# The second feed-forward product as seven half-size block products in fp16

## The chip, the cores and the metric

The kernel runs on one core of a Trainium2 chip. The metric is the time of one execution on the device, in microseconds (us). "TensorE clock" is the clock that the chip granted to the matmul engine, 1.0 being full speed. Each run is named fast or slow: slow when it lies over 1.5% above the fastest run of the same kernel. Unless a slow run is named, all comparisons here use fast runs.

## The reference

Attention over 8 batches of 8 heads (576 positions, 64 channels, a causal mask by blocks of 64), whose output is turned into 4608 rows of 512 channels. Then comes a feed-forward layer with a gate:

```python
x = np.ascontiguousarray(attn_out.transpose(0, 2, 1, 3)).reshape(B * S, H * D)   # 4608 x 512
h = x @ w_in                                                                      # 512 -> 2048
g = h * (1.0 / (1.0 + np.exp(-beta * h)))
return (g @ w_out).astype(np.float32)                                             # 2048 -> 512
```

## The kernel before

The program is laid out by a planner in the kernel file. It gives each operation to an engine, with a priority and an estimated duration, lets a small model run ahead of the chip, and fixes from that the order of every engine's instructions and the semaphores between them. Each engine then works through its list in that order: e9 and e16, two profiles of one program, have the same list of instructions on each engine, though a load landed 2.8 us later in one. TensorE's list is a mixture: attention steps come first, and pieces of feed-forward work stand between them so that TensorE has something to do while it waits for an exponential or a copy. So a change of one operation can shift the whole order.

The rows are handled in nine chunks of 512. For each chunk:

```python
for j in range(NJ):                                   # 16 tiles of the 2048 inner channels
    # TensorE: h.T = w_in.T @ x.T, four matmuls of 512 columns
    z = g.matmul(PS[:, ph.slot, :], w_in[:, c, 128 * j:128 * j + 128], xT[:, c, ...], ...)
    # ScalarE: tanh;  VectorE: (tanh + 1) * h, which frees the bank
    g.activation(th[tt.slot][:], PS[:, ph.slot, :], ACT.Tanh, scale=beta[:, j:j + 1])
    g.scalar_tensor_tensor(out=gT[tg.slot][:, j, :], in0=th[tt.slot][:], scalar=1.0,
                           in1=PS[:, ph.slot, :], op0=ALU.add, op1=ALU.mult)
# ... (cut)
for w, d0, d1 in ...:                                 # four tiles of 128 rows
    for j in range(j0, j1):                           # 16 tiles in pieces of four
        z = g.matmul(PS[:, po.slot, 0:d1 - d0], gT[tg.slot][:, j, 128 * w:128 * w + 128],
                     w_out[:, j, d0:d1], start=(j == 0), stop=(j == NJ - 1))
    # ScalarE: ost = 0.5 * PS, then the store
```

The second loop is what the change rewrites: 64 matmuls of 512 columns in bf16, in one accumulation bank at a time. The last 128 rows of the kernel are cut in two halves so that the end is short. The loads for attention pass through six buffers for q and k (`ST`) and two for v (`Vs`), which GpSimd casts to bf16. Up to 50 us of the plan, idle stretches of TensorE are filled with dummy matmuls of 256 columns (`NFILL, TFILL = 400, 50000.0`).

The softmax here doesn't subtract the row's maximum and nothing guards it: scores larger than these inputs give would overflow.

## Time and profile before

| | kernel before |
|---|---|
| time, median of 3 | 353.59 us (353.36 to 353.8) |
| profiled span | 350.3 us |
| TensorE, VectorE, ScalarE, GpSimd busy | 97, 47, 60, 22% |
| TensorE clock in the profiled run | full speed to the end of the work |

The lines that carry the argument are quoted in the prediction. In a table of stretches, the columns are the stretch in us, its length, the busy time (and number of instructions) of TensorE, its weight loads, VectorE, ScalarE and GpSimd, then the TensorE clock, the transfers' share of their engines and GB/s. This is the emptiest stretch of the kernel before after the first 50 us:

```profile
108.20:111.60 3.40, 2.47 (x18) 1.02 (x15) 1.25 (x4) 2.54 (x3) 1.45 (x2) 1.00 0.93 240
```

TensorE works 2.47 us of 3.40, or 73%.

### The profile page before, as it was taken

What the parts mean: (1) busy time and instruction counts of PE and PEld (TensorE: products, weight loads), DVE (VectorE), ACT (ScalarE), POOL (GpSimd) and SP (SyncE); (2) the same over time, 40 slices, a digit from 0 to 9 for tenths busy, and PEclk for the clock granted to TensorE, in tenths of its full rate; (3) what the DMA queues carried; (4) which work ended last, traced back from release to release, by engine and by line L of the source; (5) the groups of instructions that cost most, each with busy time, mean ns of one, the idle gap of its engine ahead of it and who ended that gap; (6) DMA issues with size and microseconds to landing.
All of it is one profiled execution on the core that took longest, in us unless ns stands there. A gap on an engine that the chain in (4) does not pass through costs nothing.

```text
span 350.3 us, 6832 instructions
## 1 busy us (share of the span) xinstructions
PE 340.2 (97%) x2809; PEld 171.1 (49%) x2753; DVE 163.8 (47%) x371; ACT 211.8 (60%) x315; POOL 78.5 (22%) x112
## 2 busy tenths in 40 slices
PE   7898999999998999999999999999999999999997
PEld 5474455445445445545445444544544444444444
DVE  4758783257123764745425453554343334424300
ACT  2937962496375896687677766768455355444521
POOL 7577260144044044044005300400000000000000
PEclk9999999999999999999999999999999999999999
DMA  7999999989989988999859797861110010010013
GB/s 206 221 239 231 193 174 203 213 202 205 238 207 209 214 189 188 231 217 199 184 146 153 184 210 167 179 127 44 34 62 31 30 62 30 30 60 32 30 37 115
DMA packets 146671, 51.88 MB, mean 148 GB/s; under 512 B 134720, under 2 KB 142160, under 8 KB 146640
## 3 DMA queue, kind: packets, MB, share of 16 engines
q1 hardware_dynamic: 135744, 37.64, 52.7%
q0 software_dynamic: 5568, 4.36, 8.2%
q10 hardware_dynamic: 5328, 9.44, 7.4%
q8 instruction: 22, 0.36, 0.4%
q14 instruction: 9, 0.07, 0.1%
HBM read 36.71 MB, written 9.44 MB: 132 GB/s over the span
## 4 chain that ended last, share of the span: by engine, by line
PE 89%; DVE 4%; ACT 3%; DMA 2%; issue 1%; SPq 0%; POOL 0%; POOLq 0%; ACTq 0%
PE PS L843 35%; PE PS L810 33%; PE PS L668 7%; PE PS L720 7%; PE PS L764 2%; DMA QKT<-QKn 2%; DVE gT L824 2%; ACT th L820 2%; PE PS L494 2%; PE PS L496 1%; ACT E L682 1%; DVE QKT L608 1%; PE PS L600 1%; DVE xq L739 1%; ACT xT L772 0%
## 5 line engine op out<-in xcount | busy, mean ns | idle before, releaser
L810 PE MATMUL PS<-xT,w_in 128*128 128x512 bf16 x576 | 140.8, 380 | 1.7 <-DVE gT L824 0.8
L843 PE MATMUL PS<-w_out,gT 128*128 128x512 bf16 (+1 forms) x592 | 139.8, 374 | 0.0
L824 DVE SCALAR_TENSOR_TENSOR gT<-th,PS 128x512 bf16<-128x512 f32 x144 | 97.2, 684 | 79.8 <-ACT th L820 78.6
L820 ACT ACTIVATE th<-PS,beta 128x512 f32<-128x512 f32 x144 | 97.8, 696 | 59.7 <-PE PS L810 58.9
L682 ACT ACTIVATE E<-PS 128x1024 bf16<-128x1024 f32 x93 | 92.0, 1029 | 27.6 <-PE PS L668 27.4
L843 PEld LDWEIGHTS PS<-w_out,gT 128*128 128x128 bf16 x592 | 55.3, 98 | 61.8 <-issue 2.1
L810 PEld LDWEIGHTS PS<-xT,w_in 128*128 128x128 bf16 x576 | 53.0, 98 | 63.3 <-issue 2.1
L855 ACT ACTIVATE ost<-PS 128x512 f32<-128x512 f32 (+1 forms) x37 | 21.7, 589 | 41.6 <-PE PS L843 41.6
L630 POOL CAST QKn<-ST 128x640 bf16<-128x640 f32 x48 | 34.7, 722 | 51.5 <-DMA ST<-in_k_dram 30.4
L668 PE MATMUL PS<-QKT 64*128 64x192 bf16 (+4 forms) x328 | 37.0, 297 | 1.6 <-DVE xq L739 1.0
L543 POOL CAST Vn<-Vs 128x2560 bf16<-128x2560 f32 (+2 forms) x11 | 18.5, 1684 | 85.8 <-DMA Vs<-in_v_dram 85.6
L720 PEld LDWEIGHTS PS<-Vn,E 128*128 128x128 bf16 x930 | 31.8, 97 | 6.5 <-issue 0.2
L720 PE MATMUL PS<-Vn,E 128*128 128x65 bf16 x930 | 32.8, 193 | 0.0
L688 DVE MEMSET E<- 64x64 uint32 x62 | 6.9, 112 | 47.2 <-ACT E L682 46.6
L668 PEld LDWEIGHTS PS<-QKT 64*128 64x128 bf16 (+1 forms) x328 | 13.4, 95 | 30.7 <-issue 15.2
L739 DVE TENSOR_TENSOR xq<-PS,inv 128x640 bf16<-128x640 f32 x32 | 26.3, 823 | 0.9
L608 DVE COPY QKT<-PS 128x576 bf16<-128x576 bf16 x16 | 11.8, 754 | 3.3 <-PE PS L600 3.1
L732 DVE RECIPROCAL inv<-PS 128x10 f32<-128x10 f32 x32 | 7.0, 218 | 12.7 <-PE PS L720 12.6
L591 POOL CAST QKn<-ST 96x768 bf16<-96x768 f32 x14 | 11.6, 830 | 3.3 <-DMA ST<-in_k_dram 2.4
L774 DVE COPY xT<-PS 128x64 bf16<-128x64 bf16 (+2 forms) x40 | 9.6, 285 | 5.6 <-PE PS L764 5.5
L690 DVE MEMSET E<- 64x128 uint32 x31 | 5.1, 165 | 14.8 <-ACT E L682 13.8
L764 PE MATMUL PS<-identB,xq 128*128 128x128 bf16 (+1 forms) x100 | 10.5, 216 | 0.3 <-DVE xq L739 0.3
(44 smaller groups left out, 76.1 us busy)
## 6 DMA issues: line engine op xcount, KB each, us to landing
out_dram<-ost ACTq DMA_DIRECT2D x35, 256.0 KB, 2.6
Vs<-in_v_dram SPq DMA_DIRECT2D x28, 256.0 KB, 4.2
ST<-in_q_dram SPq DMA_DIRECT2D x48, 128.0 KB, 2.8
ST<-in_k_dram SPq DMA_DIRECT2D x48, 128.0 KB, 2.9
ST<-in_q_dram SPq DMA_DIRECT2D x8, 288.0 KB, 6.6
ST<-in_k_dram SPq DMA_DIRECT2D x8, 288.0 KB, 7.0
w_in<-in_moe_w_in_dram POOLq DMA_DIRECT2D x4, 512.0 KB, 11.0
w_out<-in_moe_w_out_dram POOLq DMA_DIRECT2D x4, 512.0 KB, 10.9
```

The lines of the kernel that those rows point to most:

```text
L543: return g.tensor_copy(Vn[t.slot][:, 0:n, g0:g1, 0:64], Vs[ts.slot][:, 0:n, g0:g1, :])
L630: return g.tensor_copy(QKn[tn.slot][:].rearrange("p a w n -> p (a w n)")[:, 640 * (2 * a + w):][:, 0:640] .rearrange("p (t h d) -> p t h d ...
L668: z = g.matmul(o, QKT[tqk.slot][r, p, 1, 128 * t:128 * t + m], x)
L682: return g.activation(E3[es_(te)][:, g0, :, :], PS[:, ps.slot:ps.slot + 2, :], ACT.Exp, scale=0.125)
L720: z = g.matmul(o, eblk(te, t, i, h), Vn[Tv.slot][:, t, 2 * c + h, 0:65], start=(t == 0), stop=(t == i))
L739: return g.tensor_tensor(xq[tx.slot][:].rearrange("p i (h d) -> p h i d", h=2), both(pv, 0, 64), x, ALU.mult)
L764: z = g.transpose(PSb[:, px.slot, 128 * i:128 * i + r], xq[tx.slot][0:r, i, :], identB[0:r, 0:r])
L810: z = g.matmul(PS[:, ph.slot, :], w_in[:, c, 128 * j:128 * j + 128], xT[:, c, row % RX:row % RX + RC], start=(c == 0), stop=(c == 3))
L820: return g.activation(th[tt.slot][:], PS[:, ph.slot, :], ACT.Tanh, scale=beta[:, j:j + 1])
L824: return g.scalar_tensor_tensor(out=gT[tg.slot][:, j, :], in0=th[tt.slot][:], scalar=1.0, in1=PS[:, ph.slot, :], op0=ALU.add, op1=ALU.mult)
L843: z = g.matmul(PS[:, po.slot, 0:d1 - d0], gT[tg.slot][:, j, 128 * w:128 * w + 128], w_out[:, j, d0:d1], start=(j == 0), stop=(j == NJ - 1))
L855: return g.activation(ost[to.slot][:, 0:n], PS[:, po.slot, 0:n], ACT.Copy, scale=0.5)
```

## The change

The intent is to do the second product with fewer multiplications. A chunk's product A·B (A is 512x2048, B is 2048x512) is split into quarters and computed as seven half-size products instead of eight, in Winograd's form of Strassen's method:

- S1 = A21+A22, S2 = S1−A11, S3 = A11−A21, S4 = A12−S2, per chunk, on VectorE;
- T1 = B12−B11, T2 = B22−T1, T3 = B22−B12, T4 = B21−T2, once;
- p1 = A11·B11, p2 = A12·B21, p6 = S2·T2, p7 = S3·T3, p5 = S1·T1, p3 = S4·B22, p4 = A22·T4;
- C11 = p1+p2, C12 = p1+p6+p5+p3, C21 = p1+p6+p7+p4, C22 = p1+p6+p5+p7.

The products p1, p6, p5, p3 add up in one bank, which is read out after each of them; p7 and p4 share another. The first chunk keeps the plain product. The values and weights become fp16, meant to give the sums more bits. The sums lie over two of the q/k buffers and one v buffer, so later loads have fewer. The core of the diff:

```diff
+f16 = mybir.dt.float16
+        FAST = range(1, NRC)
+        OV = sb("OV", [128, 5120], f32)                 # lies over ST[4:6] and Vs[1]
+        TW = {k: OVh[:, k - 2] for k in (2, 3, 4)}
+        SW = {k: OVh[:, k + 1] for k in (2, 3)}
-        gT = [sb(f"gT{i}", [128, NJ, RC], bf16) for i in range(2)]
+        gT = [sb(f"gT{i}", [128, NJ, RC], f16) for i in range(2)]
-        w_out = sb("w_out", [128, NJ, DM], bf16)
+        w_out = sb("w_out", [128, NJ, DM], f16)
 ... (cut)
+                tw[k] = P.op("DVE", dve_t(1024), mk(lambda g, o=o, x=x, y=y: g.tensor_tensor(o, x, y, ALU.subtract)),
+                             deps=old + list(tw.values()), prio=0.6)            # four weight sums, once
 ... (cut)
+                return P.op("DVE", dve_t(SZ * HC / 2), mk(lambda g: g.tensor_tensor(
+                    fo(), fx(), fy(), op)), deps=deps, tiles=tiles, prio=prio)  # eight sums a chunk
 ... (cut)
+                for w in range(2):                       # one product: 2 row tiles x 8 tiles, 256 columns
+                        for j in range(HJ):
+                            x = g.matmul(PS[:, ps.slot, HM * w:HM * w + HM], fa()[:, j, 128 * w:128 * w + 128],
+                                         fb()[:, j, :], ...)
 ... (cut)
+            p1 = prod(Z, lambda: G(0, 0), lambda: quad(w_out, 0, 0), lo + wl, [], True, False)
+            z1 = evac(Z, oz, p1)                          # ScalarE
+            p2 = prod(W, lambda: G(0, 1), lambda: quad(w_out, 1, 0), hi + wh, [], True, True)
+            c11 = evac(W, oz, p2 + [z1], add=oz)          # VectorE, adds
 ... (cut: p6, p7, p5, p3, p4 in this order, each read out in turn)
+            if r in FAST:
+                fast(r, row, tg, gs)
+                continue
-            for w, d0, d1 in [(w, 0, DM) for w in range(4 if r < NRC - 1 else 3)] + (
-                    [] if r < NRC - 1 else [(3, 0, DM // 2), (3, DM // 2, DM)]):
+            for w, d0, d1 in [(w, 0, DM) for w in range(4)]:
```

## The prediction

> **What bounds the kernel now.** I read the page first (busy shares, slices, chain), then the chain of work in order of time, then the busy time of each engine in chosen stretches, then the timeline of the end.
>
> From the page of the kernel before:
>
> ```profile
> PE 340.2 (97%) x2809; PEld 171.1 (49%) x2753; DVE 163.8 (47%) x371; ACT 211.8 (60%) x315; POOL 78.5 (22%) x112
> ...
> PE 89%; DVE 4%; ACT 3%; DMA 2%; issue 1%; SPq 0%; POOL 0%; POOLq 0%; ACTq 0%
> ...
> L843 PE MATMUL PS<-w_out,gT 128*128 128x512 bf16 (+1 forms) x592 | 139.8, 374 | 0.0
> L824 DVE SCALAR_TENSOR_TENSOR gT<-th,PS 128x512 bf16<-128x512 f32 x144 | 97.2, 684 | 79.8 <-ACT th L820 78.6
> ```
>
> TensorE is busy 97% of the span and carries 89% of the chain that ended last. L843, the second feed-forward product that the change rewrites, is 35% of that chain. But the 374 ns of one matmul is a latency of pipelined work, so what a matmul costs has to come from spacing. The chain in order of time gives it: each row chunk of 512 rows ends in the same piece, and the pieces repeat exactly.
>
> ```profile
> 249.22 4.32 PE PS L843 x20
> ...
> 276.85 4.32 PE PS L843 x20
> ...
> 304.47 4.32 PE PS L843 x20
> ...
> 332.10 15.59 PE PS L843 x88
> ```
>
> The period is 27.63 us. A chunk has 64 matmuls of the first product and 64 of the second, all with 512 columns, so one costs 27.63 / 128 = **215.9 ns**, with not a nanosecond of waiting in the sum. The end of the kernel also has 32 matmuls with 256 columns (the last output rows are cut in halves). In the timeline of the end:
>
> ```profile
> 331.94 15.74 PE L843 MATMUL PS<-w_out,gT 128*128 128x512 bf16 x88
> ...
> 347.72 0.38 ACT L855 ACTIVATE ost<-PS 128x256 f32<-128x256 f32 x1 [1.31 <-PE PS L843]
> ```
>
> The last of the 88 starts some 15.47 us after the first (15.74 less its own 0.27). 56 of the gaps are wide ones, 56 x 0.2159 = 12.09; the other 31 take 3.38 us, or **109 ns** each. So half-width matmuls, each with its own weight load (98 ns in the page), keep their pace: the load stays hidden.
>
> The stretches show where TensorE has slack and how full VectorE is (columns: PE, PEld, DVE, ACT, POOL busy us):
>
> ```profile
> 40.00:80.00 40.00, 38.59 (x340) 19.61 (x332) 21.29 (x50) 24.82 (x38) 13.26 (x14) 1.00 1.03 199
> 80.00:120.00 40.00, 39.07 (x356) 19.63 (x344) 16.65 (x45) 24.64 (x35) 11.05 (x14) 1.00 0.99 215
> 120.00:160.00 40.00, 40.00 (x377) 19.91 (x364) 23.78 (x64) 30.30 (x46) 13.60 (x15) 1.00 0.93 206
> ...
> 276.85:304.47 27.62, 27.62 (x129) 12.54 (x128) 11.00 (x16) 13.38 (x20) 0.00 (x0) 1.00 0.10 39
> ```
>
> From 120 us on TensorE never stops; before, it loses 2.3 us in 80 while the transfers are full (DMA share 1.03 and 0.99). Attention and its loads end near 248 us, and over three and a half chunks of feed-forward work are then left, so slower loads in the middle would be hidden. VectorE has room everywhere: 60% at its fullest, 40% late.
>
> [...]
>
> **The change part by part**, per chunk, for eight of nine chunks.
>
> TensorE. Removed: 64 wide matmuls, 64 x 215.9 = 13.82 us. Added: seven products, each of 2 row tiles x 8 k-tiles with 256 columns, 112 x 109 = 12.21 us. Saving 1.61 us, not the full eighth (1.73)[...]. Eight chunks: 12.9 us at most. Fp16 should cost no more than bf16.
>
> VectorE. Added: eight sums of 1024 fp16 elements. [...]one is an estimated 690 ns; eight are 5.5 us. Four evacuations move to it, each like the 684 ns row of L824: 2.7. Together 8.3 us a chunk, 66 in all, and once four weight sums of 1.22 us, 4.9. VectorE goes from 164 to some 235 us, 69% of the new span; a late chunk from 11 to 19.3 us of 26; around 120 to 160 us, where a chunk takes some 34 us, from 60% to some 84%. It does not become the bound, but matmul banks will be freed a little later.
>
> ScalarE. Three evacuations for four, 0.6 us less a chunk. Neutral.
>
> Buffers. The new sums lie over two of six q/k staging buffers and one of two v buffers, which later loads then lack. Before, the casts wait for the loads (QKn for k 30.4 us, Vn for v 85.6), not the loads for the casts, so this should show little, except early.
>
> Banks. One accumulating bank is held nearly the whole chunk and a second half of it, where before one output bank was held at a time. While attention lasts, four banks serve feed-forward work, so the first product often has two. One use of a bank is matmuls 0.86 + tanh 0.70 + product on VectorE 0.68, with gaps some 2.5 us, so two banks supply one tile per 1.25 us; TensorE needs one per 1.6 (late) to 2. Just enough: I allow 1.5 us of stalls in all.
>
> Where the saving doesn't arrive. Chunk 1's product runs near 88 to 112 us, when TensorE has nothing but this product to fill with until the next batch's attention is through; I give away half of it, 0.8. In the last chunk, the sequence p5, read of the bank, p3 has a wait of some 0.9 us with no next chunk to fill it (perhaps a left-over of chunk 7); the last evacuation is 0.75 us on VectorE in place of 0.38 on ScalarE; and the last store is 256 KB instead of 128 (2.6 for 1.9 us in the page's issues). So of its 1.6 about 0.5 remains.
>
> Sum: chunks 2 to 7 give 6 x 1.61 = 9.7; chunk 1 0.8; the last 0.5; together 11.0. Less stalls of 1.5: 9.5. 353.6 - 9.5 = 344.1 us.
>
> **The rivals.** (a) **VectorE becomes the bound**: [...] Against it: the rate of the xT copies. Blocking by GpSimd casts (13.6 of 40 us busy there) is the milder form. It would eat 5 to 10 us: 349 to 354. (b) **Banks and in-order waits**: partial sums are read between products, so a late evacuation stops TensorE, which is in order. For it: two or three free banks in the attention stages. Against: late chunks have all eight, and between the products of one chunk lie those of the next. Up to 5 us: 349. (c) **Starved by transfers**: fewer staging buffers while DMA is full. For it: the DMA share of 1.0 to 120 us. Against: the large stock of feed-forward work after 160. It could lose chunks 1 and 2 and some more: 347. (d) **Nothing lost**: 353.6 - 12.9 = 340.7.
>
> **Range and chances.** I weigh the plain sum with small stalls 0.65, (d) 0.1, (a) to (c) 0.25 together. That gives 344.1, range 340.8 to 350.0. Faster by over 2% means below 346.5: 0.74. Within 2%: 0.23. Slower: 0.03.
>
> **What would show it.** In the chain, late chunks with a period of 26.0 us, not 27.63; if it is more, TensorE waits for VectorE or ScalarE and names the line. 896 matmuls with 256 columns. The fp16 sums at 690 ns in the groups by shape; 1.2 us would mean rival (a). TensorE's idle time in 40 to 120 us up from 2.3 by about 1 to 2, and under 1 us from 120 to 250; more with a releaser in VectorE means (b), in DMA or casts (c). The end, from the last tanh to the last store, no more than half a us shorter. The prediction is wrong above all if half-width fp16 matmuls don't keep 109 ns over long runs, or if VectorE's queue delays the products that free the banks.

What the trace of the kernel before has for these estimates, by shape: two matmuls of 256 columns cost 2.1 ns more than one of 512 (2 x 109 against 215.9). The 16-bit copies to xT took 283 ns for 256 elements and 420 for 512, or 0.54 ns an element; at this pace a sum would take an estimated 694 ns for 1024 elements and 1.24 us for 2048. Two f32 operations of VectorE took 684 ns for 512 elements (L824) and 823 for 640 (L739); at their pace a sum of 1024 would take an estimated 1.24 us, which is rival (a). The profile of e1 later had 695 ns for the sums within `gT` and 1.22 us for the weight sums.

## The result

The changed kernel took 350.64 us in the median of five runs (349.75 to 356.78, the highest a slow run), against 353.64 us (353.36 to 354.52) for the kernel before in the same rounds. The ratio of the fast runs is 0.9892 (95% interval 0.985 to 0.9935), which counts as the same within 2%. A ratio here is the mean time of one kernel's fast runs over the mean of the other's fast runs of the same rounds, so it isn't quite the ratio of the medians. The measured 350.64 lies outside the predicted range of 340.8 to 350.0, and 6.5 us above the predicted 344.1. The prediction was wrong. In two later batches the same kernel took 349.57 and 348.28 us in the median, beside 352.94 and 353.83 for the kernel before. These two lie inside the range, but the gain, 3.0, 3.4 and 5.6 us in the three batches, is well under the predicted 9.5 in each.

The profile taken with this result was of the slow run. I read a second profile of the same kernel (350.70 us, span 348.9), the first of the experiments. From its page: busy times, the clock in 40 slices, the shares of the chain that ended last, and three groups.

```profile
PE 331.4 (95%) x3177; PEld 207.5 (59%) x3121; DVE 225.1 (65%) x463; ACT 212.2 (61%) x314; POOL 79.6 (23%) x110
...
PEclk9999999999999998999999999999999999999999
...
PE 78%; DVE 5%; ACT 5%; DMA 4%; SPq 3%; POOL 2%; issue 2%; ACTq 0%; POOLq 0%
...
L879 PE MATMUL PS<-w_out,gT 128*128 128x256 f16 x512 | 65.5, 273 | 0.7 <-ACT ost L893 0.7
...
L896 DVE SCALAR_TENSOR_TENSOR ost<-PS,ost 128x512 f32<-128x512 f32 x24 | 16.4, 685 | 18.0 <-PE PS L879 16.2
L846 DVE TENSOR_TENSOR OV<-gT 128x1024 f16<-128x1024 f16 x32 | 24.5, 774 | 1.1 <-PE PS L879 0.6
```

TensorE's share of the chain fell from 89% to 78%: the end is now reached through more waits on other engines. VectorE stands at 225 us, near the predicted 235, and is no bound. One slice has a lower TensorE clock. The sums at L846 take 774 ns in the mean, not 690.

The late chunks are exactly as predicted. From the chain in order of time (start, length, engine, what, line, count) and the table of stretches:

```profile
277.56 5.24 PE PS L879 x48
...
303.60 5.24 PE PS L879 x48
...
329.63 11.37 PE PS L879 x104
341.68 3.68 PE PS L879 x32
```

```profile
277.56:303.60 26.04, 26.04 (x178) 17.19 (x177) 17.61 (x28) 13.39 (x20) 0.00 (x0) 1.00 0.12 41
```

The period is 26.04 us, for 27.63 before, and TensorE doesn't stop in it. So a narrow fp16 matmul costs (26.04 − 64 x 0.2159) / 112 = 109 ns, and each full chunk saves 1.59 us. The saving is real; it was lost elsewhere. To see where, I added up TensorE's lost time in each trace: the distances between the starts of consecutive matmuls, less the usual distance of that pair of kinds (215.9 and 109 ns within the feed-forward work; between kinds, the lower quartile over the traces). Stretches at half clock count as lost too. For two profiles of the changed kernel and, for later use, one of a kernel with other filling (e13):

| us lost, by time of the start | before | changed, e1 | changed, e17 | e13 |
|---|---|---|---|---|
| to 40 us (loads, start) | 8.5 | 9.5 | 8.7 | 8.2 |
| 40 to 80 | 2.1 | 2.1 | 2.1 | 1.3 |
| 80 to 120 (chunk 1's product) | 1.4 | 2.4 | 3.9 | 1.6 |
| 120 to 140 | 0.2 | 4.3 | 1.8 | 0.9 |
| 140 to 240 | 1.0 | 1.9 | 1.8 | 2.7 |
| 240 to 330 | 0.0 | 1.3 | 1.1 | 0.1 |
| 330 to the last matmul | 0.0 | 0.9 | 0.9 | 0.9 |
| sum | 13.2 | 22.3 | 20.3 | 15.6 |
| last matmul's start to the end of the span | 2.9 | 3.8 | 3.8 | 3.8 |
| span | 350.3 | 348.9 | 346.9 | 343.4 |

The changed kernel saves 12.9 us of matmuls at full pace (560 at 215.9 ns and 32 at 109 make 124.4 us; 64 and 896 make 111.5) and loses 7.1 to 9.1 us more in holes, 0.9 of it in the tail, 0.2 to 1.0 at the start, and most of the rest between 80 and 140 us and around 240. Another 0.96 us goes to a longer end. Some 1.5 us of both differences I can't place; it lies in the switches between kinds of matmul, which this reckoning takes as given.

The largest hole of e1, from its timeline (start, length, engine, line, operation, and the idle time before it with its releaser):

```profile
125.77 2.32 POOL L558 CAST Vn<-Vs 128x2560 bf16<-128x2560 f32 x1 [12.35 <-DMA Vs<-in_v_dram]
...
125.84 2.79 DVE L846 TENSOR_TENSOR OV<-gT 128x1024 f16<-128x1024 f16 x1
...
128.94 1.08 PE L737 MATMUL PS<-Vn,E 128*128 128x65 bf16 x30 [1.66 <-DVE E L707]
```

One cast of v starts on GpSimd, and 0.07 us later a sum starts on VectorE. The sum takes 2.79 us instead of 0.69. Behind it in VectorE's list stands a small memset of the exponentials (L707), on which TensorE's next attention step waits, so TensorE stops for 1.66 us. Then comes the second part:

```profile
127.10:130.50 3.40, 1.74 (x38) 1.26 (x38) 2.97 (x6) 1.30 (x4) 2.55 (x3) 1.00 0.92 200
130.50:133.90 3.40, 3.40 (x8) 0.94 (x8) 2.06 (x5) 1.83 (x3) 1.45 (x2) 0.50 0.66 147
```

TensorE was busy only half of one stretch of 3.4 us (1.74 of 3.40), and in the next one it gets half its clock: 8 wide matmuls took the time of 16, a further 1.7 us. In e17 the same happens around the spot that was emptiest before the change:

```profile
108.20:111.60 3.40, 1.76 (x34) 1.08 (x28) 1.90 (x7) 1.35 (x2) 1.44 (x2) 1.00 1.10 297
111.60:115.00 3.40, 3.20 (x34) 2.24 (x35) 1.36 (x5) 1.05 (x2) 1.45 (x2) 0.50 1.24 242
```

And the end of e1, with ScalarE reading the bank between p5 and p3:

```profile
341.02 0.60 ACT L893 ACTIVATE ost<-PS 128x512 f32<-128x512 f32 x1 [2.02 <-PE PS L879]
341.65 0.69 DVE L896 SCALAR_TENSOR_TENSOR ost<-PS,ost 128x512 f32<-128x512 f32 x1 [1.68 <-ACT ost L893]
...
341.68 1.05 PE L879 MATMUL PS<-w_out,gT 128*128 128x256 f16 x8 [0.69 <-ACT ost L893]
...
345.38 0.69 DVE L896 SCALAR_TENSOR_TENSOR ost<-PS,ost 128x512 f32<-128x512 f32 x1 [3.04 <-PE PS L879]
```

TensorE waits 0.69 us for the read of p5, and after the last product there is an addition of 0.69 us on VectorE and a 256 KB store. That is the wait I had seen coming, but 0.9 + 0.96 us of it in all, more than the chunk's whole saving of 1.6.

### The profile page after: what moved, and what is told of

It reads as the page before. It is cut to its first block, busy times and chain, and to the rows that moved or that the text cites.

```text
span 354.6 us, 7617 instructions
## 1 busy us (share of the span) xinstructions
PE 332.2 (94%) x3140; PEld 209.7 (59%) x3121; DVE 227.1 (64%) x463; ACT 212.6 (60%) x314; POOL 80.4 (23%) x110
## 4 chain that ended last, share of the span: by engine, by line
PE 75%; DVE 6%; DMA 6%; ACT 4%; SPq 3%; issue 3%; POOL 2%; POOLq 0%; ACTq 0%
PE PS L946 31%; PE PS L879 26%; PE PS L737 6%; PE PS L685 5%; PE PS L982 4%; ACT th L956 2%; ACT E L699 2%; DMA ST<-in_q_dram 2%; DMA QKT<-QKn 2%; DVE gT L960 2%; DMA Vs<-in_v_dram 2%; PE PS L781 2%; SPq L532 2%; DVE gT L846 1%; DVE w_out L828 1%
## 5 line engine op out<-in xcount | busy, mean ns | idle before, releaser
L960 DVE SCALAR_TENSOR_TENSOR gT<-th,PS 128x512 f16<-128x512 f32 x144 | 97.0, 683 | 43.8 <-ACT th L956 43.3
L879 PE MATMUL PS<-w_out,gT 128*128 128x256 f16 x512 | 65.5, 273 | 0.7 <-ACT ost L893 0.7
L879 PEld LDWEIGHTS PS<-w_out,gT 128*128 128x128 f16 x512 | 48.5, 98 | 14.4 <-ACT ost L893 1.5
L685 PE MATMUL PS<-QKT 64*128 64x512 bf16 (+4 forms) x328 | 38.0, 303 | 6.5 <-ACT E L699 3.2
L893 ACT ACTIVATE ost<-PS 128x512 f32<-128x512 f32 x32 | 19.2, 600 | 26.4 <-PE PS L879 26.3
L879 PE MATMUL PS<-OV 128*128 128x256 f16 x256 | 34.4, 282 | 0.4 <-DVE OV L828 0.4
L879 PEld LDWEIGHTS PS<-OV 128*128 128x128 f16 x256 | 25.4, 101 | 8.6 <-DVE OV L828 0.5
L896 DVE SCALAR_TENSOR_TENSOR ost<-PS,ost 128x512 f32<-128x512 f32 x24 | 16.4, 685 | 18.1 <-PE PS L879 16.2
L846 DVE TENSOR_TENSOR OV<-gT 128x1024 f16<-128x1024 f16 x32 | 22.7, 716 | 1.1 <-PE PS L879 0.6
L879 PE MATMUL PS<-OV,gT 128*128 128x256 f16 x128 | 16.6, 273 | 0.0
```

What stands on the lines that cost most here:

```text
L685: z = g.matmul(o, QKT[tqk.slot][r, p, 1, 128 * t:128 * t + m], x)
L846: return P.op("DVE", dve_t(SZ * HC / 2), mk(lambda g: g.tensor_tensor(fo(), fx(), fy(), op)), deps=deps, tiles=tiles, prio=prio)
L879: x = g.matmul(PS[:, ps.slot, HM * w:HM * w + HM], fa()[:, j, 128 * w:128 * w + 128], fb()[:, j, :], start=first and w == 0 and j == 0, st ...
L893: return P.op("ACT", act_t(DM) + 80, lambda g, e: g.activation(ost[to.slot][:], PS[:, ps.slot, :], ACT.Copy, scale=0.5), deps=deps, tiles= ...
L960: return g.scalar_tensor_tensor(out=gT[tg.slot][:, j, :], in0=th[tt.slot][:], scalar=1.0, in1=PS[:, ph.slot, :], op0=ALU.add, op1=ALU.mult)
```

## The experiments

The theory after this reading: **VectorE's queue and the clock.** The sums, lengthened by casts that run at the same time, hold up small attention steps on VectorE; TensorE, which is in order, stops (1.66 us in e1); and a stop that empties one stretch of 3.4 us (1.74 us busy in e1) is followed by one at half clock. Rivals (these are new ones; the prediction's have letters): **staging**, fewer buffers for q, k and v, so that loads come late; **chunk 1**, whose product is the only filling around 100 us, so that starting one chunk later would give all back; and **the tail** alone. The runs came in five batches, each with its own runs of the kernel before.

### The first batch: repeat, undo, and cut the sums

**e1_after_again** is the changed kernel, unaltered.

> The changed kernel unaltered, for a profile in the fast state. All theories: about 350.2 us, 3 us under the kernel before. The changeover theory (the loss of some 6 us sits between 80 and 130 us, where the first weight sums and chunk sums queue on VectorE with GpSimd casts) expects TensorE idle there to be about 5 us more than before, and under 1.5 us more elsewhere; the spread theory (VectorE too full in the whole attention stage) expects it evenly from 80 to 250 us.

It took 349.57 us in the median of four runs (347.94 to 350.70), ratio 0.9881 (0.9821 to 0.9942). So the result repeats. Its profile is read above.

**e2_plain_all** keeps fp16, the overlaid buffers and the fourth output buffer, but makes no chunk of seven products:

```diff
-        FAST = range(1, NRC)
+        FAST = range(NRC, NRC)
 (and the last rows cut in halves, as before)
```

> No chunk with the seven products, but all else of the change stays: fp16, the sums' room laid over two q/k staging buffers and one v buffer (nothing is written there), four output buffers. The staging theory (the lost buffers cost the missing 6 us) expects 358 to 360 us, 5 to 6 over the kernel before. The changeover and the spread theories expect 353 to 354.5, as before.

354.48 us, ratio 1.0031 (0.9963 to 1.0099), correct. Fp16 in place of bf16 costs nothing that shows. The interval is too wide to size the buffers; e8 repeats it.

**e3_tiny_weight_sums** cuts the four weight sums to two columns each and leaves the order of all instructions as it was. The result is wrong.

```diff
-g.tensor_tensor(o, x, y, ALU.subtract)
+g.tensor_tensor(o[:, :, 0:2], x[:, :, 0:2], y[:, :, 0:2], ALU.subtract)
 (the products read quarters of w_out where they read T2, T3, T4)
```

> Wrong result on purpose. Order of all instructions and waits as in the changed kernel; only the four weight sums are cut to 2 columns of 256 (16 elements for 2048), and the products read the raw quarter of the weights. Changeover theory, in the form that the weight sums are the culprit: 345 to 347 us, some 4 us faster than the changed kernel. Spread and staging theories: within 1 us of the changed kernel, 349 to 350.5.

349.15 us, ratio 0.9884 (0.9835 to 0.9934): no gain over e1. The length of the weight sums isn't what was lost; the expected gain was a miss. A half-clock stretch remained, at 112.6 us.

**e4_tiny_all_sums** cuts the per-chunk sums to two columns too, with the same order, and is wrong.

```diff
-                    fo(), fx(), fy(), op))
+                    fo()[:, :, 0:2], fx()[:, :, 0:2], fy()[:, :, 0:2], op))
```

> Wrong result on purpose. As the one with small weight sums, and all sums of activations are cut to 2 columns as well (8 elements for 1024), so VectorE is freed of all sums with the order unchanged. Spread theory: 343 to 345 us, near the 344 that the prediction had. Changeover theory with the weight sums as culprit: no more than 1 us below the run with small weight sums. Staging theory: 349 to 350, no gain.

346.98 us, ratio 0.9832 (0.9779 to 0.9885), 2.6 us less than e1. So in this batch the length of all the sums together looks worth some 2 to 3 us, but the intervals overlap, and the unaltered kernel reached the same ratio (0.9833) on another chip in e17: this is not shown. But even with sums of almost no length the kernel doesn't come to 344: a half-clock stretch followed the hole at 108 to 112 us here as well, and one of the sums shows that a cast can lengthen even a sum of eight elements:

```profile
126.30 1.62 DVE L846 TENSOR_TENSOR OV<-gT 128x8 f16<-128x8 f16 x1
```

Eight elements took 1.62 us; the mean of these small sums is 0.25 us. A cast of v had begun at 125.59 and lasted 2.32 us, and the sum ended with it.

### The second batch: contention, the first chunk, GpSimd, staging

**e5_memset_sums** puts memsets of the same length in place of the sums. They read no operand in SBUF, and no lengthening shows in them: both groups of 32 have a mean of 688 ns, and each of the four for the weight sums took 1225 ns.

```diff
-mk(lambda g: g.tensor_tensor(fo(), fx(), fy(), op))
+mk(lambda g: g.memset(fo()[:, :, 0:189], 0.03))
```

> Wrong result on purpose. Order and waits of the changed kernel; each sum (weights and activations) is a memset of about the same length, some 0.7 us for a sum of activations, so VectorE is as busy as in the changed kernel but reads nothing from SBUF for the sums[...]. Theory that contention with the casts is what the sums cost: 346 to 347 us, at least as fast as the run with all sums small (347.0), because there even small sums waited for casts (one took 1.6 us). Theory that it is VectorE's occupancy: 349 to 350, as the changed kernel.

350.36 us (348.44 to 353.23), ratio 0.9915 (0.9878 to 0.9951). That is no better than the changed kernel, so lengthening by casts alone can't be the cause. The profile shows two half-clock stretches, after stretches with TensorE busy for 58 and 51%. The holes are there with sums of plain length.

The hole at 108 to 112 us doesn't depend on the sums' length at all. The least busy 3.41 us between 100 and 115 us are 46% full in e1, e3, e4, e5 and e17 alike, and in e17 no sum runs there. TensorE waits until VectorE has scaled the attention output (`xq`). Before the change, four wide matmuls of chunk 1's product stood in this wait. First the kernel before, then e17:

```profile
107.54 1.03 PE L843 MATMUL PS<-w_out,gT 128*128 128x512 bf16 x4
108.88 0.39 PE L668 MATMUL PS<-QKT 64*128 64x512 bf16 x2 [0.31 <-DVE xq L739]
```

```profile
107.81 1.08 PE L737 MATMUL PS<-Vn,E 128*128 128x65 bf16 x30
110.07 0.39 PE L685 MATMUL PS<-QKT 64*128 64x512 bf16 x2 [1.18 <-DVE xq L756]
```

So this hole is missing filling, and not a sum in the way. Whether chunk 1's shorter product or the new order takes it away wasn't tried apart.

**e6_from_third** starts one chunk later.

```diff
-        FAST = range(1, NRC)
+        FAST = range(2, NRC)
```

> The seven products from the third chunk on, the second chunk plain. Theory that the second chunk's saving never arrives (TensorE runs dry near 108 us whatever the second chunk costs, because the third waits for its batch) and that the first sums make it worse: 348 to 349.5 us, as fast as the changed kernel or up to 1.5 us faster, with TensorE idle between 80 and 140 us by some 2 us less. Rival, that each chunk's saving counts: 351 us, 1.6 slower.

352.82 us, ratio 0.9986 (0.9962 to 1.0009): 3 us worse than the changed kernel, where one chunk's saving is at most 1.6. The chunk-1 rival in its simple form missed. The holes did not go away; the two deepest, 1.9 us at 110.5 and 2.1 us at 239.1 by the reckoning of lost time, were each followed by a half-clock stretch (from 112.9 and 242.6). All six runs had a clock of 0.990 or lower.

**e7_pool_sums** moves the per-chunk sums to GpSimd, except in the last chunk.

```diff
-                return P.op("DVE", dve_t(SZ * HC / 2), ...
+                return P.op("POOL" if r < NRC - 1 else "DVE", 1100 if r < NRC - 1 else dve_t(SZ * HC / 2), ...
```

> The sums of activations on GpSimd in place of VectorE in all chunks but the last. If contention and occupancy on VectorE cost some 2.5 us, and a sum takes GpSimd about 1.1 us (an estimate from its casts, 0.72 us for 640 elements): 347 to 348 us. If the sums are slower than 2 us there, they will hold the casts up and the products that need them: over 350.

357.49 us, ratio 1.0078 (1.0036 to 1.012), worse than before the change. The sums there took twice the time that I had planned for:

```profile
L846 POOL TENSOR_TENSOR OV<-gT 128x1024 f16<-128x1024 f16 x28 | 60.3, 2154 | 44.5 <-DVE gT L960 26.9 <-PE PS L879 16.0
```

The groups have 2.12 to 2.24 us, or some 2.1 ns an element; the 1.1 us was an estimate from the casts, which take 1.13 ns an element (0.72 us for 640). And the contention only changed sides: three of the four weight sums on VectorE, beside sums on GpSimd, took 2.5 to 3.1 us instead of 1.22.

**e8_plain_all_again** is e2 with more rounds.

> A repeat of the run without the seven products, for a narrower interval: 354.5 was measured beside 352.9 for the kernel before. Theory that the two lost staging buffers and the lost v buffer cost 1 to 3 us: a ratio of 1.003 to 1.008, and a hole in TensorE of about 1 us between 240 and 260 us where it waits for the last transposed loads. Theory that they cost nothing: a ratio within 0.998 to 1.002.

353.87 us, ratio 1.0007 (0.9974 to 1.0039). In time the smaller staging costs less than the scatter. In the trace it does show. The order of TensorE's instructions is that of the kernel before, instruction for instruction, and there are two new holes, at 231 and 237 us. The second:

```profile
238.96 0.39 PE L685 MATMUL PS<-QKT 64*128 64x512 bf16 x2 [1.14 <-DMA QKT<-QKn]
```

TensorE lost 2.2 us in 220 to 240 us, against 0.3 before. The same wait on the transposing transfer of the last batch is in e1 (1.13 us at 244.6). So the staging rival is right in kind for some 1 to 2 us, late in attention, and no more.

### The third batch: fill the hole, start later, mend the tail

**e9_fill_the_hole** lets the planner put dummy matmuls into idle stretches up to 135 us of the plan. It adds 23 of 256 columns, 20 of them near 108 to 113 us, and its order of everything after differs.

```diff
-        NFILL, TFILL = 400, 50000.0
+        NFILL, TFILL = 600, 135000.0
```

> The changed kernel with 20 dummy matmuls of 256 columns (2.2 us at 109 ns) put among the attention work near 108 to 113 us, where TensorE ran dry in the profiles. Theory that holes of some 2 us make the clock drop to half for 3.4 us and that this costs up to 1.7 us: full clock from 100 to 120 us, and 348 to 349 us if no other hole drops it. Rival, that the clock plays no part: 349.6 or slower by the dummies. The order behind them shifts, so a second drop near 130 us may stay; the clock of the profiled run will say.

348.02 us (345.78 to 349.2), ratio 0.9825 (0.9787 to 0.9863), correct, and the clock was between 0.998 and 1.0 in all six runs.

**e10_from_fourth** starts with the fourth chunk, when there is more feed-forward work in stock.

```diff
+        FAST = range(3, NRC)
```

> The seven products from the fourth chunk on, so that the weight sums and the first sums come after 140 us, when TensorE has a stock of feed-forward work. Stock theory (until some 140 us TensorE has nothing to put in the place of a late attention step, so that each delay on VectorE becomes a hole, and a hole halves the clock): no drop of the clock, holes between 80 and 140 us as in the kernel before (1.6 us by the sum of gaps, against 6.6 in the changed kernel's fast profile), and 346.5 to 348.5 us although 3.2 us of saving are given up. Rival, each chunk's saving counts wherever it is: 352.8.

351.33 us, ratio 0.9925 (0.9886 to 0.9964), a miss. The stretch from 80 to 140 us is then nearly as before the change (1.8 us lost, for 1.6), but 2.2 us are lost in new holes between 180 and 200, where the four weight sums now sit, again against a cast of v:

```profile
184.24 2.32 POOL L558 CAST Vn<-Vs 128x2560 bf16<-128x2560 f32 x1 [18.40 <-DMA Vs<-in_v_dram]
...
184.71 2.92 DVE L828 TENSOR_TENSOR OV<-w_out 128x2048 f16<-128x2048 f16 x1
```

The disturbance moves with the first chunk of seven products; starting later doesn't avoid it. Three of the six runs had a clock of 0.99.

**e11_from_fourth_plain_last** is e10 with the last chunk plain, its end in halves. The quarter B12 is changed in place, so its result is wrong (relative error 0.14). I take the timing to stand; that the values do not matter to it isn't shown by a run.

```diff
+        FAST = range(3, NRC - 1)
```

> As the run from the fourth chunk, and the last chunk plain with its end halved as in the kernel before. Tail theory (the last chunk's saving of 1.6 us is eaten by a hole of 0.85 us and a longer last evacuation and store of about 1.0): within 0.7 us of the run from the fourth chunk. Rival: 1.6 us slower than that.

349.55 us, ratio 0.9882 (0.9854 to 0.991), all six runs at full clock. The three full-clock runs of e10 have a mean of 349.95, these six of 349.69. So nothing of the last chunk's 1.6 us shows, though three and six runs spread over 1.5 and 2.3 us can't exclude a part of it. The traces say the same: its tail takes back 0.9 + 0.96 us.

**e12_from_fourth_split_end** keeps the last chunk's seven products, but puts p7 and p4 into two banks in halves, so that additions and stores of the end are half as large.

```diff
+  Y = (P.tile("P1"), P.tile("P1"))     # in the last chunk (this cut is shortened)
+  for w in range(2):                   # the last two additions and stores, in halves; the last store by SyncE
+      P.op("DVE", dve_t(HM), ... ost[to.slot][:, c], in0=PS[:, ps[w].slot, c] ...)
```

> As the run from the fourth chunk, with the last chunk's final two evacuations and stores in halves over two banks, so that the end is 256 columns on VectorE (about 0.42 us) and a store of 128 KB. If the longer last evacuation and store cost about 1.0 us: 0.7 to 1.0 us faster than the run from the fourth chunk, and the time from the last matmul's start to the end near 2.9 us where the changed kernel has 3.8.

350.56 us (two of the six runs slow; the four fast ones have a mean of 349.95), ratio 0.9889 (0.9856 to 0.9921), so no gain over e10 that shows. The last matmul's start to the end took 4.17 us, against 3.67 in e10: the last store, of 128 KB, was issued at 343.73 and took 3.0 us to land. A miss.

### The fourth batch: what the filling does

**e13_two_column_fill** is e9 with dummies of 2 columns in place of 256, so that they fill an order but hardly any time.

```diff
+  g.matmul(PS[:, tf.slot, 0:2], identB[:], identW[:, 0:2])     # planned after 60 us
```

> Order and waits exactly as in the run with dummy matmuls in the hole, but the 20 dummies near 108 to 113 us have 2 columns for 256, so TensorE is idle there again. Theory that the clock is what that run gained: the clock drops to half once near 110 to 117 us and the time goes back up by 1 to 2 us, to 349 to 350. Rival, that the changed order behind the dummies gained it: no change, 348.

348.29 us, ratio 0.9811 (0.9752 to 0.987). The gain stayed, so it isn't the dummies' work that does it; I had expected it to go. What the profile shows is another order, in which the hole at 108 to 112 us holds other work: TensorE was busy 2.57 of the 3.40 us from 108.2 (0.49 of it only the small dummies), for 1.76 in e17. Its profiled run took 345.23 us, the fastest of its six and 1.1 above the prediction; the median is 4.2 above it.

**e14_fill_tiny_sums** joins e9 and e4 (wrong).

> Wrong result on purpose. Dummy matmuls in the hole, and all sums (weights and activations) cut to 2 columns, the order as in the run with the dummies. If holes left by VectorE's sums and the clock's drop are separate causes that add: 345 to 346 us, 2 to 3 under the run with the dummies, and within 2 us of the 344.1 that the prediction had. If they are one cause: 348.

348.20 us, ratio 0.9821 (0.9753 to 0.989). With this order the sums' length is worth nothing that shows; the two gains don't add up.

**e15_fill_plain_last** is e9 with a plain last chunk, and one more VectorE operation that turns B12 back, so its result is right.

```diff
+        FAST = range(1, NRC - 1)
+                    quad(w_out, 0, 1), quad(w_out, 0, 1), quad(w_out, 0, 0), ALU.add)), deps=[tw[1], tw[2], *used], ...
```

> Correct. Dummy matmuls in the hole, and the last chunk plain with its end halved as before (one more sum on VectorE turns the changed quarter of the weights back). A candidate for the best version. Tail theory: 346.5 to 348, the same as the run with the dummies or up to 1.5 us faster. If the last chunk's saving counts: 349.6.

349.17 us, ratio 0.9809 (0.9738 to 0.9879; the median includes two slow runs). The same as e9 again: nothing to be had in the tail either way.

**e16_fill_again** is the same program as e9.

> The run with the dummies again, beside the three others on their chip: 348 us, full clock through all runs.

348.52 us (one of the six runs slow), ratio 0.9829 (0.9768 to 0.989). It repeats e9 in time, and the two profiles show how much is chance. First e9, then e16, around 96 us, with the same list of instructions on each engine:

```profile
95.61 1.22 DVE L828 TENSOR_TENSOR OV<-w_out 128x2048 f16<-128x2048 f16 x1
...
98.04 2.47 POOL L558 CAST Vn<-Vs 128x2560 bf16<-128x2560 f32 x1 [12.53 <-DMA Vs<-in_v_dram]
```

```profile
95.21 2.38 POOL L558 CAST Vn<-Vs 128x2560 bf16<-128x2560 f32 x1 [11.82 <-DMA Vs<-in_v_dram]
95.33 3.34 DVE L828 TENSOR_TENSOR OV<-w_out 128x2048 f16<-128x2048 f16 x1
...
98.73 2.88 PE L879 MATMUL PS<-OV 128*128 128x256 f16 x16 [1.51 <-DVE OV L828]
```

In e9 the load of v landed 2.8 us later, and the weight sum, 1.22 us long, was over before the cast began. In e16 the cast was first by 0.12 us, the sum took 3.34, TensorE waited for it, and the clock followed:

```profile
96.10:99.50 3.40, 1.51 (x17) 1.01 (x16) 3.30 (x4) 2.59 (x5) 1.57 (x2) 1.00 1.10 257
99.50:102.90 3.40, 3.40 (x38) 2.85 (x36) 0.99 (x3) 0.60 (x1) 2.88 (x4) 0.50 1.01 211
```

The spans were 346.0 and 349.0 us. This is the clearest pair: one program, one meeting of a cast and a sum more, 3 us. (By the reckoning of lost time, 3.2 us of it lie between 80 and 120 us; other stretches differ by up to 1.4 us either way and nearly cancel.) That the cast comes first was set by a transfer's landing, 2.8 us apart in the two, which the same order of instructions did not fix.

### The fifth batch: is any version better?

**e17_after_third** is the changed kernel again, and **e18_fill_plain_last_again** is e15, both on a third chip.

> The changed kernel once more, beside the candidate for the best version on the same chip: 349 to 350.5 us and a ratio near 0.989, with one or two drops of the clock in most runs.

> The candidate for the best version again (dummy matmuls among the attention work near 108 to 113 us, last chunk plain): 1 to 2.5 us faster than the changed kernel of the same rounds, 347 to 349.

e17: 348.28 us (346.30 to 350.81), ratio 0.9833 (0.9786 to 0.988). e18: 348.45 us, ratio 0.9845 (0.9793 to 0.9897). So the filling that looked 1 to 2 us better in other batches isn't better here. No version beats the changed kernel in a way that repeats. An interval that crosses 0.98 in the table leaves open whether that run is faster by 2% or the same.

| run | median us | ratio to before | 95% |
|---|---|---|---|
| changed kernel (three batches) | 350.64, 349.57, 348.28 | 0.9892, 0.9881, 0.9833 | see above |
| e2, e8 plain, fp16 and smaller staging | 354.48, 353.87 | 1.0031, 1.0007 | .9963–1.0099, .9974–1.0039 |
| e3 weight sums cut | 349.15 | 0.9884 | .9835–.9934 |
| e4 all sums cut | 346.98 | 0.9832 | .9779–.9885 |
| e5 memsets for sums | 350.36 | 0.9915 | .9878–.9951 |
| e6 from the third chunk | 352.82 | 0.9986 | .9962–1.0009 |
| e7 sums on GpSimd | 357.49 | 1.0078 | 1.0036–1.012 |
| e9, e16 filled | 348.02, 348.52 | 0.9825, 0.9829 | .9787–.9863, .9768–.989 |
| e13 filled, two columns | 348.29 | 0.9811 | .9752–.987 |
| e10, e12 from the fourth | 351.33, 350.56 | 0.9925, 0.9889 | .9886–.9964, .9856–.9921 |
| e11 from the fourth, last plain | 349.55 | 0.9882 | .9854–.991 |
| e14 filled, sums cut | 348.20 | 0.9821 | .9753–.989 |
| e15, e18 filled, last plain | 349.17, 348.45 | 0.9809, 0.9845 | .9738–.9879, .9793–.9897 |

### The clock, read over all profiles

No run was made for this; it is a reading of the twenty traces there are. In a trace with two half-clock stretches, their starts lie a whole number of 3.413 us apart, to 0.02 us: 98.38 and 115.44 in e5 (5 times), 112.86 and 242.56 in e6 (38 times). The profile of the slow run has three, 6.827, 3.413 and 3.413 us long, from 14.40, 103.15 and 120.21 us (26 and 5 times). So in these traces the clock changes on a fixed grid of 3.413 us. For 19 of the profiles a half-clock stretch, if only that after the end of the work, gives the position of the grid, and I took TensorE's busy share in every cell of it after 38 us:

| busy share of a cell | cells | followed by a half-clock cell |
|---|---|---|
| up to 0.514 | 13 | 12 |
| 0.52 to 0.60 | 7 | 1 |
| over 0.60 | all others | 0 |

So TensorE needn't be idle for a whole cell: of the 13 cells with TensorE busy for up to 51%, 12 were followed by 3.41 us at half clock. The clock records of the kernel before and of the slow run have two states, full and half.

This may also be why equal programs differ. Taking every position of a 3.41 us window, the least busy one between 100 and 115 us is 73% busy before the change, and 46% in five profiles of the unaltered order (e1, e3, e4, e5, e17). Whether a cell falls on that hole differs from run to run with the grid's position. In e1 none did (the cell there had 58%), and the hole at 127 us was caught, with half clock from 130.5; in e17 one did, with half clock from 111.6. Among the 14 fast runs of the changed kernel, the five at a clock of 0.998 or more have a mean of 347.8 us, the eight at 0.995 a mean of 350.0, and one at 0.988 took 349.8. One stretch of 3.41 us at half clock makes a mean clock of 0.995 over 348 us.

## Why the prediction was wrong

By its own steps:

- **A narrow matmul at 109 ns: right.** 896 of them, a late period of 26.04 us against the foretold 26.0, TensorE without a stop in late chunks. Fp16 cost nothing that shows (e2 and e8: ratios of 1.0031 and 1.0007), and the results were right (e1, e17) although a bank is read in the middle of its sum.
- **VectorE's load: right.** 225 us for the foretold 235; sums of 690 ns where no cast ran, weight sums of 1.22 us. Rival (a) as a bound fell. Its milder form, casts that block sums, is real (2.79 us for a sum beside a cast in e1).
- **"I allow 1.5 us of stalls in all": this step failed.** The term was mis-sized. Outside the tail, and with the start left out, the lost time grew by 6.0 us (e17) to 7.2 us (e1). The prediction had 1.5 for stalls and 0.8 for chunk 1, so 3.7 to 4.9 us were missing. I had derived the stalls from banks alone, at the average pace. The traces show three things in their place that the average hides. The sums stand in VectorE's in-order list ahead of small attention steps that TensorE waits for, and a cast makes one sum 2.8 to 3.3 us long (TensorE stopped for 1.66 us in e1, 1.51 in e16). The emptiest spot, 73% full before, fell to 46% because filling was gone from it, whatever the sums' length (e3, e4, e5). And a cell of the clock's grid that is half empty cost another 1.7 us (e1, from 130.5 us: 8 wide matmuls in the time of 16). The prediction didn't consider the clock at all. The late wait on loads gave 1.1 to 1.3 us of the sum.
- **"So of its 1.6 about 0.5 remains" (the last chunk): failed.** Its own terms, a wait of 0.9, 0.37 more for the last evacuation (0.75 was my estimate, 0.69 measured) and 0.7 more for the store, add up to 2.0. The 0.5 holds only if left-over work of chunk 7 fills the wait, and nothing did. The hole and the longer end took 0.9 + 0.96 us, all of it; e11 against e10, at full clock, shows no difference between seven products and the plain one there.
- **Chunk 1 at half its saving: not settled.** In 80 to 120 us TensorE lost 1.0 us more than before in e1 and 2.5 in e17, of which 1.7 is the clock. Without the clock that is what I gave away, 0.8. But e6, which leaves chunk 1 plain, was 3 us slower; in its trace two weight sums of 1.51 and 1.73 us start at 109.49 and 110.93, in the same hole, and the copy that TensorE's next product needs comes after them.
- **Rival (b), banks and in-order waits: half right.** Between 60 and 270 us TensorE of e1 never waited for a partial sum to be read, and for a bank's product (`gT`) it waited 1.2 us, 0.6 more than before. The order on VectorE did hold it up, but at attention's steps.
- **Rival (c), loads: right in kind and small**, some 1 to 2 us near 240 us, where I had expected it early.

The causes add up: full-pace saving 12.9, less 6.0 to 7.2 outside the tail, less 1.8 in the tail and end, less the 1.5 not placed, gives 2.4 to 3.6 us before differences of the start (e1's start lost 1.0 us more, e17's 0.2); the spans of e1 and e17 are shorter than before by 1.4 and 3.4. That the sums' length matters as a whole is suggested by e4 and not borne out by e14 and e17. That a cast's meeting with a sum costs time is shown by one pair of profiles, e16 against e9. That the clock's grid decides part of the scatter is read from all the traces, not tried. Two things stay open. The share of each cause isn't fixed, as taking one away (e3, e5, e14) brought nothing or little while others remained. And why the order of e9 and e13 loses less before 140 us, but gains nothing lasting against the changed kernel of e17, would take many more runs than the scatter of 1 to 4 us between runs of one program allowed here.

## What to carry to other kernels

Here the saving in matmuls arrived where TensorE was full (1.59 us in a late chunk), and was lost where it waited now and then (4.3 us lost in e1 from 120 to 140 us, for 0.2 before). For such a place, look up the emptiest stretch of a few us in the trace before, not the mean, and ask two things: what the new work on other engines will put in front of the small steps that TensorE waits for, and whether the matmuls saved were the filling there. If a change can push TensorE below half in a stretch of 3.4 us, add a half-clock stretch of 1.7 us to the sum (12 of 13 such cells had one behind them here). And for the last piece of a kernel, count reads, additions and stores to the end by themselves: a form with dependent steps can lose there all that it saves (here 0.9 + 0.96 us of 1.6).
